# Top-k attention and an ELU feed-forward block on one core: the first two weight pieces on GpSimd's queue, half decoded in the prologue

## The chip, the core and the metric

The kernel runs on one core of a Trainium2 chip. A core has five engines with their own instruction streams: TensorE (PE; its weight loads are shown as PEld), VectorE (DVE), ScalarE (ACT), GpSimd (POOL) and SyncE (SP, which here only issues DMAs). They meet through semaphores. Sixteen DMA engines move data between HBM and the on-chip memory. The metric is the time of one execution on the device, in microseconds; lower is better.

## The reference

```python
# q, k, v: (8, 8, 576, 64)
scores = scale * np.matmul(q, k.transpose(0, 1, 3, 2))
kth = np.partition(scores, -32, axis=-1)[..., -32:-31]
scores = np.where(scores >= kth, scores, -1e9)
attn = softmax(scores)
x = (attn @ v) laid out as (4608, 512)
h = x @ w_in                      # w_in (512, 2048)
g = np.where(h > 0, h, np.exp(np.minimum(h, 0)) - 1)
out = g @ w_out                   # w_out (2048, 512)
```

All arrays but the two weights arrive as 32-bit floats. `w_in` and `w_out` arrive as 64-bit floats, and the kernel turns them into 32-bit floats itself, which is the decoding that this case is about.

## The kernel before

**Attention.** A step of the kernel is one tile of 128 queries (or the 64 left over, for two pairs of heads) of one batch, with one pair of heads. `load_qk` and `load_v` issue the DMAs of a head pair; `transpose_qk` turns q and k on PE and copies them back on ACT (L264, L277); `scores` multiplies them on PE (L301) and copies the result to a tile `sc` on ACT (L309). `select_row` and, later, `select` find the 32 largest of each row on DVE: four times the top eight (MAX8 on L320/L330 or L343/L355) with three replacements between them (L324 or L348). `mask` turns the row into exponentials: two small operations on POOL (L368, L370) and two on ACT (L371, L372). `normalise` works out the reciprocal of the sum on POOL and scales there (L382 to L389). `turn` transposes the result on PE (L408) and copies it on ACT (L409), and `attend` multiplies with v (L434) and puts the result into `xT` (L461).

**Feed-forward.** When a block of tokens has its `xT`, `ffn_pieces` queues its pieces: `hidden` (PE L502, ACT L510 to L513) and `project` (PE L523), with the gate finished on DVE (L478). `feed` takes pieces from this queue four times a step, when the planner's credit allows and when enough weight pieces are decoded (`decoded[0]`).

**Weights.** There are 32 pieces of 128 x 512 numbers, 16 of `w_in` and 16 of `w_out`. `load_weight(i)` fetches the 512 KB of 64-bit words into one of five buffers `raw`, on SP's queue. `convert_first(i)` is the first half of the decoding: three operations on ACT (L170 to L172) and one on POOL (L173). `convert_last(i)` is the second half: two on DVE (L180, L183) and an addition on POOL (L187) that writes `w_in` or `w_out`. `decode_piece(i)` loads piece i + 2, does the first half of piece i and the second half of piece i - 2. Such calls wait in the list `decode`, 34 of them, and `hook` runs one of them at each point in the selection where it is called: twice a step in the first four steps, six times a step in the next four, and three times a step from step 8. When the list is empty, the buffers `raw` are given up for those of the later feed-forward blocks.

**Order.** The first eight steps (`tight = 2 * NHP`) are left to a scheduler of the framework, which may move an instruction of an engine ahead of others when its inputs allow it. Inside `manual_schedule` (a stretch of the prologue that holds the transposes and scores of the first two steps, and everything from step 8 on) the instructions keep the order in which they are written, but those from outside can still be put between them. Each engine then runs its instructions strictly in the order that results, so that one which waits holds up all behind it.

**The prologue.** L628 loads q and k of head pair 0 (k on SP's queue, q on ACT's), L629 weight piece 0, L630 q and k of head pair 1, L631 weight piece 1 and L632 v of head pair 0. L633 to L637 hold the transposes and scores of the first two steps. Then the other q, k and v of batch 0 follow, and L642 fills the list `decode`.

Of the kernel before, what the change touches and what calls it, by code (L numbers as in the profile page):

```python
# [80 lines left out]
def kernel(  # L81
# [9 lines left out]
    nc = tc.nc  # L91
# [9 lines left out]
    NF = dff // P  # L101
# [36 lines left out]
    WN = 512  # L138
    raw = {}

    def weight(i):
        per = dff // WN
        if i < NC * per:
            f, c = divmod(i, NC)
            src = moe_w_in[c * P : (c + 1) * P, 2 * f * WN : 2 * (f + 1) * WN]
            return src, w_in[:, c, f * WN : (f + 1) * WN]
        f = i - NC * per
        return moe_w_out[f * P : (f + 1) * P, :], w_out[:, f, :]

    def load_weight(i):  # L150
        t = rawpool.tile([P, 3 * WN], U32, tag="raw", name="raw")
        nc.sync.dma_start(t[:, 0 : 2 * WN], weight(i)[0])
        raw[i] = t

    def parts(t):
# [3 lines left out]
    def convert_first(i):  # L159

        lo, hi, e = parts(raw[i])
        ef, mf = e.bitcast(FP32), lo.bitcast(FP32)
        nc.scalar.activation(ef, hi.bitcast(FP32), AF.Abs, scale=2.0**-48)  # L170
        nc.scalar.activation(mf, lo, AF.Copy, scale=2.0**-29, bias=2.0**23)
        nc.scalar.activation(lo.bitcast(I32), mf, AF.Copy, bias=-(2.0**23))  # L172
        nc.gpsimd.tensor_scalar(  # L173
            ef, ef, (2.0 - 2.0**-3 - 2.0**-23) * 2.0**-32, 2.0**-63, ALU.min, ALU.max
        )

    def convert_last(i):
        t, dst = raw.pop(i), weight(i)[1]
        lo, hi, e = parts(t)
        nc.vector.tensor_scalar(  # L180
            e, e, 0x0FFFFFFF, 3, ALU.bitwise_and, ALU.logical_shift_left
        )
        nc.vector.scalar_tensor_tensor(  # L183
            out=e, in0=hi, scalar=0x80000000, in1=e,
            op0=ALU.bitwise_and, op1=ALU.bitwise_or,
        )
        nc.gpsimd.tensor_tensor(  # L187
            dst.bitcast(I32), e.bitcast(I32), lo.bitcast(I32), ALU.add
        )

    decode = []
# [13 lines left out]
    def decode_piece(i):  # L205
        if i < 2 * NF:
            if i + 2 < 2 * NF:
                load_weight(i + 2)
            convert_first(i)
        if i > 1:  # L210
            convert_last(i - 2)
            decoded[0] = i - 1
# [3 lines left out]
    def load_qk(b, hp, other=nc.sync):  # L216

        for name, src in (("k", k), ("q", q)):
            n, queue = (J + 1, nc.sync) if name == "k" else (J, other)
            t = ldpool.tile([P, n, 2, D], FP32, tag=name + "in", name=name + "in")  # L220
            if name == "k":
                last = t
            for hh in range(2):
                queue.dma_start(
                    t[:, 0:J, hh, :],
                    src[b, 2 * hp + hh, 0:JP, :].rearrange("(p j) d -> p j d", j=J),
                )
            queue.dma_start(
                last[0:R, J, :, :] if name == "k" else last[R:P, J, :, :],
                src[b, 2 * hp : 2 * hp + 2, JP:S, :].rearrange("h p d -> p h d"),  # L230
            )
            loaded[b, hp, name] = t

    def load_v(b, hp):

        t = kvpool.tile([P, 2 * J + 2, D], FP32, tag="vT", name="vT")
        for hh in range(2):
            h = 2 * hp + hh
            nc.sync.dma_start(
                t[:, hh * J : (hh + 1) * J, :],  # L240
                v[b, h, 0:JP, :].rearrange("(p j) d -> p j d", j=J),
            )
            mine = slice(hh * R, (hh + 1) * R)
            other = slice((1 - hh) * R, (2 - hh) * R)
            nc.gpsimd.memset(t[other, 2 * J + hh, :], 0.0)
            nc.sync.dma_start(t[mine, 2 * J + hh, :], v[b, h, JP:S, :])
        vT[b, hp] = t
# [32 lines left out]
    def start_qk(b, hp):  # L280
        turning.append(transpose_qk(b, hp))

    def turn_qk(whole=False):
        while turning:
            if next(turning[0], turning) is turning:
                turning.pop(0)
            elif not whole:
                return
# [3 lines left out]
    def scores(u):  # L292

        u.sc = scpool.tile([P, 2, S], FP32, tag="sc", name="sc")
        q0 = QUERIES + u.t.qt * P
        for half in range(2):
            for h, i, rows in u.heads:
                kq = kqT[u.t.b, h // 2]
                part = slice(i * D, (i + 1) * D)
                k0 = (KEYS if i == 0 else 0) + half * HS  # L300
                nc.tensor.matmul(  # L301
                    wide[i][rows, half, 0:HS],
                    kq[part, q0 : q0 + u.t.ql],
                    kq[part, k0 : k0 + HS],
                    start=True,
                    stop=True,
                )
        for i in range(2):
            nc.scalar.activation(  # L309
                u.sc[:, i, :].rearrange("p (a s) -> p a s", a=2),  # L310
                wide[i][:, :, 0:HS], AF.Copy, scale=scale,
            )
# [239 lines left out]
    for b in range(B):  # L552
# [12 lines left out]
        for qt in range(J + 1):  # L565
# [8 lines left out]
            t = Tile(b, qt, rows, blk, slice(c0, c0 + n))  # L574
# [21 lines left out]
    def at(step, fn, *args):  # L596
        todo.setdefault(step, []).append((fn, args))
# [28 lines left out]
    E = mybir.EngineType  # L626
    engines = {E.PE, E.Activation, E.DVE, E.Pool}
    load_qk(0, 0, nc.scalar)  # L628
    load_weight(0)  # L629
    load_qk(0, 1)  # L630
    load_weight(1)  # L631
    load_v(0, 0)  # L632
    with tc.manual_schedule(engines=engines):  # L633
        for hp in range(2):
            start_qk(0, hp)
            turn_qk(True)
            scores(steps[hp])  # L637
    load_qk(0, 2)
    load_qk(0, 3)
    for hp in range(1, NHP):  # L640
        load_v(0, hp)
    decode += [lambda i=i: decode_piece(i) for i in range(2 * NF + 2)]  # L642
    at(0, start_qk, 0, 2)
    at(1, start_qk, 0, 3)

# [92 lines left out]
```

## Time and profile before

| | us |
|---|---|
| median of 3 runs (lowest, highest) | 1682.49 (1682.45, 1682.61) |
| the profiled execution | 1682.55 |
| its span, first to last instruction | 1680.8 |
| busy in the span: PE, DVE, ACT, POOL | 1604.5, 1534.4, 1167.5, 638.8 |
| first 15 us, busy: PE, DVE, ACT, POOL | 4.77, 1.54, 6.25, 3.81 |
| 15 to 60 us, busy: PE, DVE, ACT, POOL | 39.41, 44.97, 34.53, 23.16 |
| last 81 us, busy: PE, DVE | 76.73, 5.54 |
| start of step 4's selection on DVE | 58.05 |
| start of step 8's selection on DVE | 146.48 |
| start of step 9's selection on DVE | 158.59 |
| weight loads, issue to landing, lowest, median, highest | 3.1, 3.9, 8.0 |

The busy times are sums of the instructions' durations on each engine, so an engine whose sum is near the length of a stretch has no room in it. A start in the lower rows is the start of the first MAX8 of that step on DVE. A line of a timeline gives start, duration, engine, source line, operation, output and input, a count, and in brackets how long the engine had been idle before it and what ended that.

### The profile page before, as it was taken

The numbers are of one execution on the slowest core, as the hardware profiler recorded it, in microseconds if no ns is written. First come the engines' busy times: TensorE is split into PE (matmuls) and PEld (weight loads), VectorE is DVE, ScalarE is ACT, GpSimd is POOL, SyncE is SP. The second block draws the span as 40 slices with busy tenths as digits, with TensorE's granted clock in tenths as the row PEclk, the third lists the DMA queues.
The fourth block names the chain that finished last, engine by engine and source line by source line (L and its number), as shares of the span: only waits on it lengthen the run. The fifth ranks groups of instructions, "written<-read, shape, count | busy, mean of one in ns | idle before, by whom it ended". The sixth has DMA issues, their size and how long they took to land.

```text
span 1680.8 us, 26396 instructions
## 1 busy us (share of the span) xinstructions
PE 1604.5 (95%) x8560; PEld 1041.7 (62%) x8560; DVE 1534.4 (91%) x3096; ACT 1167.5 (69%) x2661; POOL 638.8 (38%) x1719
## 2 busy tenths in 40 slices
PE   6767999999999999999999999999999999999999
PEld 4554776667575666656557575756558575755565
DVE  6999999999999999999999999999998999998600
ACT  6776786778776776767768685857758586857531
POOL 3776333433333334434334333333333333332200
PEclk8567999999999999999999999999999999999999
DMA  7441021001200111001200111001100000000000
GB/s 192 134 156 39 16 56 36 7 1 47 52 7 7 29 35 42 1 21 36 49 14 1 36 35 42 1 13 43 43 13 8 21 21 29 7 7 7 7 13 13
DMA packets 101129, 56.22 MB, mean 33 GB/s; under 512 B 84097, under 2 KB 92289, under 8 KB 100993
## 3 DMA queue, kind: packets, MB, share of 16 engines
q1 hardware_dynamic: 99792, 54.26, 11.6%
q8 instruction: 68, 1.11, 0.3%
q14 instruction: 69, 0.56, 0.1%
q10 hardware_dynamic: 1200, 0.30, 0.1%
HBM read 45.09 MB, written 9.44 MB: 32 GB/s over the span
## 4 chain that ended last, share of the span: by engine, by line
PE 59%; DVE 26%; ACT 5%; issue 1%; POOL 1%; ACTq 0%; DVEq 0%; POOLq 0%
PE ops L523 22%; PE hps L502 19%; DVE wk L348 11%; DVE m L355 9%; PE avps L434 7%; PE scps L301 6%; PE eps L408 4%; DVE m L343 3%; DVE gT L478 2%; ACT sc L372 1%; ACT sc L371 1%; PE qkps L271 1%; ACT et L409 1%; PE scps L408 1%; ACT n L510 0%
## 5 line engine op out<-in xcount | busy, mean ns | idle before, releaser
L502 PE MATMUL hps<-xT,w_in 128*128 128x256 f32 (+2 forms) x2432 | 557.4, 378 | 25.9 <-ACT gT L511 23.6
L355 DVE MAX8 m<-wk 128x8 f32<-128x576 f32 x816 | 574.5, 744 | 0.0
L523 PE MATMUL ops<-w_out,gT 128*128 128x512 f32 x1152 | 523.8, 599 | 0.0
L502 PEld LDWEIGHTS hps<-xT,w_in 128*128 128x128 f32 x2432 | 411.5, 195 | 127.4 <-ACT gT L511 34.4
L348 DVE MATCH_REPLACE8 wk<-m,wk 128x576 f32<-128x576 f32 x544 | 399.2, 740 | 0.0
L523 PEld LDWEIGHTS ops<-w_out,gT 128*128 128x128 f32 x1152 | 209.0, 190 | 233.6 <-issue 218.7
L382 POOL TENSOR_SCALAR dene<-den 128x2 f32<-128x2 f32 x144 | 34.8, 242 | 832.9 <-ACT sc L372 832.7
L371 ACT ACTIVATE sc<-sc,neg 128x576 f32<-128x576 f32 x288 | 226.4, 786 | 63.2 <-POOL neg L368 63.0
L372 ACT ACTIVATE sc<-sc,gap 128x576 f32<-128x576 f32 x288 | 223.2, 775 | 25.2
L309 ACT ACTIVATE sc<-scps 128x576 f32<-128x576 f32 x288 | 173.6, 662 | 76.6 <-PE scps L301 76.6
L389 POOL TENSOR_SCALAR sc<-sc,rec 128x576 f32<-128x576 f32 x288 | 219.5, 773 | 15.2 <-POOL rec L387 0.6
L409 ACT COPY et<-eps 128x512 f32<-128x512 f32 x288 | 167.5, 582 | 68.4 <-PE eps L408 68.2
L301 PE MATMUL scps<-kqT 64*128 64x288 f32 (+1 forms) x1280 | 200.5, 439 | 15.1 <-ACT kqT L277 8.3
L348 DVE MATCH_REPLACE8 wk<-m,sc 128x576 f32<-128x576 f32 x272 | 199.6, 740 | 0.0
L408 PEld LDWEIGHTS eps<-ident,sc 128*128 128x128 f32 x1152 | 145.1, 145 | 82.9 <-issue 48.0
L478 DVE SCALAR_TENSOR_TENSOR gT<-n,gT 128x512 f32<-128x512 f32 (+2 forms) x152 | 106.5, 701 | 97.7 <-ACT n L513 97.6
L434 PE MATMUL avps<-et,vT 128*64 128x256 f32 (+2 forms) x2080 | 190.4, 326 | 2.7 <-ACT et L409 2.3
L343 DVE MAX8 m<-sc 128x8 f32<-128x576 f32 x272 | 191.0, 742 | 0.0
L408 PE MATMUL eps<-ident,sc 128*128 128x128 f32 x1152 | 178.1, 281 | 12.9 <-POOL sc L389 11.9
L510 ACT ACTIVATE n<-hps 128x256 f32<-128x256 f32 (+2 forms) x304 | 112.6, 370 | 85.5 <-PE hps L502 75.0
L434 PEld LDWEIGHTS avps<-et,vT 128*64 128x64 f32 x2080 | 123.5, 141 | 73.1 <-issue 24.2
L301 PEld LDWEIGHTS scps<-kqT 64*128 64x128 f32 (+1 forms) x1280 | 107.7, 181 | 83.6 <-issue 44.8
(47 smaller groups left out, 1226.8 us busy)
## 6 DMA issues: line engine op xcount, KB each, us to landing
kin<-in_k_dram SPq DMA_DIRECT2D x64, 128.0 KB, 2.8
raw<-in_moe_w_in_dram SPq DMA_DIRECT2D x16, 512.0 KB, 4.4
vT<-in_v_dram SPq DMA_DIRECT2D x64, 128.0 KB, 2.3
raw<-in_moe_w_out_dram SPq DMA_DIRECT2D x16, 512.0 KB, 3.2
out_dram<-osb SPq DMA_DIRECT2D x32, 256.0 KB, 2.3
qin<-in_q_dram SPq DMA_DIRECT2D x62, 128.0 KB, 2.8
kin<-in_k_dram SPq DMA_DIRECT2D x32, 32.0 KB, 2.5
vT<-in_v_dram SPq DMA_DIRECT2D x64, 16.0 KB, 2.2
```

Source lines behind the costliest of these rows:

```text
L301: nc.tensor.matmul(wide[i][rows, half, 0:HS], kq[part, q0 : q0 + u.t.ql], kq[part, k0 : k0 + HS], start=True, stop=True,)
L343: nc.vector.max(found[i], cur[i])
L348: nc.vector.match_replace(wk[i], found[i], cur[i], TAKEN)
L355: nc.vector.max(found[i], cur[i])
L371: nc.scalar.activation(sc, sc, AF.Prelu, bias=neg[:], alpha=STEEP)
L372: nc.scalar.activation(sc, sc, AF.Exp, bias=gap[:], accum_out=u.den[:, i : i + 1])
L389: nc.gpsimd.tensor_scalar(u.sc[:, i, :], u.sc[:, i, :], rec[:, i : i + 1], 1.0, ALU.mult, ALU.mult)
L408: nc.tensor.transpose(ps[:, c * P : (c + 1) * P], sc[:, c0 : c0 + P], ident[:])
L409: nc.scalar.copy(g.et[:, chunks, u.at, :], ps[:, 0 : n * P].rearrange("p (c q) -> p c q", c=n),)
L434: nc.tensor.matmul(ps[i * D : (i + 1) * D, cols], vt[:, 2 * J + i if c == J else i * J + c, :], w, start=(c == 0), stop=(c == J),)
L502: nc.tensor.matmul(ps[:, 0:n_tok], w_in[:, i, f * P : (f + 1) * P], blk.xT[:, i, 0:n_tok], start=(i == 0), stop=(i == NC - 1),)
L523: nc.tensor.matmul(blk.o[:], blk.gT[f // NG][:, f % NG, s * P : (s + 1) * P], w_out[:, f, :], start=(f == 0), stop=(f == NF - 1),)
```

## The change

The loads of weight pieces 0 and 1 are issued on GpSimd's queue, both of them between the loads of q and k of head pair 0 and those of head pair 1. The calls `decode_piece(0)` and `decode_piece(1)` are made in the prologue, after the scores of step 0 and of step 1; as before, such a call loads piece i + 2 on SP's queue and does the first half of piece i. The list `decode` begins with call 2 and has 32 entries instead of 34.

```diff
-    def load_weight(i):
+    def load_weight(i, queue=nc.sync):
         t = rawpool.tile([P, 3 * WN], U32, tag="raw", name="raw")
-        nc.sync.dma_start(t[:, 0 : 2 * WN], weight(i)[0])
+        queue.dma_start(t[:, 0 : 2 * WN], weight(i)[0])
         raw[i] = t
...
     load_qk(0, 0, nc.scalar)
-    load_weight(0)
+    for i in range(2):
+        load_weight(i, nc.gpsimd)
     load_qk(0, 1)
-    load_weight(1)
     load_v(0, 0)
     with tc.manual_schedule(engines=engines):
         for hp in range(2):
             start_qk(0, hp)
             turn_qk(True)
             scores(steps[hp])
+            decode_piece(hp)
     load_qk(0, 2)
     load_qk(0, 3)
     for hp in range(1, NHP):
         load_v(0, hp)
-    decode += [lambda i=i: decode_piece(i) for i in range(2 * NF + 2)]
+    decode += [lambda i=i: decode_piece(i) for i in range(2, 2 * NF + 2)]
```

## The prediction
> **What bounds the kernel now.** I read the slices of the page first, then the busy time by stage, then the two ends of the stretch that the change touches: the timelines of ACT and DVE at the start, and the chain that ended last around 155 us.
>
> ```profile
> 60.00:165.00 105.00, 72.03 (x332) 51.38 (x332) 99.21 (x173) 78.00 (x178) 74.59 (x107) 0.70 0.34 111
> 165.00:400.00 235.00, 219.46 (x1605) 158.07 (x1604) 233.57 (x494) 174.06 (x460) 88.83 (x261) 1.00 0.10 26
> 400.00:1000.00 600.00, 594.09 (x3140) 385.26 (x3139) 593.75 (x1209) 441.60 (x986) 229.91 (x658) 1.00 0.10 27
> 1000.00:1600.00 600.00, 597.96 (x3056) 371.37 (x3053) 555.78 (x1123) 413.69 (x911) 216.49 (x626) 1.00 0.07 18
> ```
> Columns: stage, its length, then busy us of PE, PEld, DVE, ACT, POOL. DVE idles 1.4 us of 235 up to 400 us; PE is the full engine after that. The chain that ended last is DVE alone from 283 us to past 700 us and PE's from about 717 us. So a shift of DVE's work at the start travels to the end, as long as DVE stays without gaps up to there.
>
> The start, on ACT and then on DVE:
> ```profile
> 8.34 0.66 ACT L170 ACTIVATE raw<-raw 128x512 f32<-128x512 f32 x1 [4.29 <-DMA raw<-in_moe_w_in_dram]
> 10.36 1.08 ACT L277 COPY kqT<-qkps 128x512 f32<-128x512 f32 x2
> 13.09 0.66 ACT L170 ACTIVATE raw<-raw 128x512 f32<-128x512 f32 x1 [1.66 <-DMA raw<-in_moe_w_in_dram]
> 14.21 1.17 ACT L309 ACTIVATE sc<-scps 128x576 f32<-128x576 f32 x2
> ...
> 14.57 0.43 DVE L180 TENSOR_SCALAR raw<-raw 128x512 uint32<-128x512 uint32 x1 [3.67 <-POOL raw L173]
> 15.64 1.42 DVE L320 MAX8 m<-sc 128x8 f32<-128x576 f32 x2
> 109.88 1.51 DVE L180 TENSOR_SCALAR raw<-raw 128x512 uint32<-128x512 uint32 x1 [3.46 <-POOL raw L173]
> ```
> ACT stands at piece 0's decode until its load lands (8.34), with q and k already turned on PE; their copies and the first scores come after it, and selection begins at 15.64. The last line is a later wait of DVE for POOL.
>
> The chain in step 8 (start, us, what), and where it returns to DVE:
> ```profile
> 153.47 2.54 issue
> 156.02 1.28 POOL w_out L187
> ...
> 157.39 0.24 POOL dene L382
> ...
> 160.16 1.12 PE eps L408 x4
> ```
> ```profile
> 283.10 0.42 DVE L478 SCALAR_TENSOR_TENSOR gT<-n,gT 128x256 f32<-128x256 f32 x1 [1.43 <-ACT n L513]
> ```
> The last w_out piece stands on POOL ahead of step 7's normalisation, PE idles 5.15 us for it, and the chain runs over PE and ACT until DVE waits 1.43 us at 283 us.
>
> Decode on DVE up to step 9's start (158.59), and the DMA engines early on (share and GB/s last):
> ```profile
> L183 DVE SCALAR_TENSOR_TENSOR raw<-raw 128x512 uint32<-128x512 uint32 x32 | 27.3, 854 | 0.1
> L180 DVE TENSOR_SCALAR raw<-raw 128x512 uint32<-128x512 uint32 x32 | 24.1, 754 | 19.1 <-POOL raw L173 19.1
> ```
> ```profile
> 3.00:6.00 3.00, 0.25 (x2) 0.28 (x3) 0.00 (x0) 1.05 (x1) 0.00 (x0) 1.00 1.04 211
> 6.00:9.00 3.00, 2.12 (x10) 1.71 (x9) 0.00 (x0) 0.66 (x2) 0.00 (x0) 1.00 1.00 257
> ```
> Undisturbed, an L180 takes 0.41 and an L183 0.68 us, so 27.3 - 32 x 0.68 = 5.5 us, 24.1 - 32 x 0.41 = 11.0 us and some 2.3 us of L478 are stretch. Waits for L173 after 15.64 are 19.1 - 9.74 - 3.67 = 5.7 us. Together DVE loses 24.5 us to POOL before step 9, nearly all in steps 4 to 7.
>
> **What the Trainium skill says.** "SBUF — State Buffer", section "SBUF: two separate sides": some DVE operations and GpSimd share a port pair as an exclusive lock for a whole instruction. The trace agrees: an L180 at 58.71 took 1.40 us and ended with the L187 that ran on POOL from 58.54 to 59.83. "DMA: Bandwidth & Descriptors", section "Issuing engines are not separate DMA queues": whoever issues, the same 16 engines move the bytes; their share of 1.0 above says they are full from 3 to 9 us, so a second queue adds no bandwidth there. The same page, section "Queues, rings and completion order": an engine takes turns between queues by packet. Here weights have 4 KB rows, q and k 256 B runs, so POOL's loads would take most of the turns; no run shows it yet. Its section "SWDGE vs HWDGE vs iDMA": GpSimd itself writes the descriptors of its DMAs.
>
> **The change part by part.**
> *Two loads leave SP for POOL.* SP is freed of 0.60 + 0.59 us. POOL issues one load ahead of the identity's last step, which ends at 1.68 and is needed at 5.75. No row shows a POOL issue; I take 1 us for each, with 0 and 4 us as bounds, all hidden behind the next point. q and k of head pair 0 land later, by at most the 2.8 us of engine time of two weight pieces; hidden likewise.
>
> *What ACT really gets.* In the built order of the changed kernel, ACT runs L264, L277 twice, and then L170 to L172 of **piece 2**, ahead of the first scores' L309. Piece 2 is loaded by SP, after q and k of both head pairs and six loads of v. Pieces 0 and 1 do follow the scores. So the wait at the head of ACT isn't removed, it passes from piece 0 to piece 2.
> Its landing: from windows, weights move at about 372 GB/s at full share (365 at 0.98 from 30 us), small runs at about 240 (196 at 0.75, 155 at 0.69). Ahead of and with it go two times 0.59 MB of q and k (4.9 us), 0.44 MB of v (1.8 us) and three pieces of 0.52 MB (4.2 us): 10.9 us. The same sum for before, up to piece 1's landing at 13.09, gives 9.0 where the engines were busy 10.2, so times 1.14: 12.5 us from 2.2 us on, 14.7. By issue: SP has 15 issues ahead of it, of 0.5 to 0.8 us by their rows of before, so 10.1 us, or 11.5 when it waits for landings; plus 4 to 4.7 us as for piece 1: 14.1 to 16.2. I take 15.4, bounds 13.6 and 19. From L170's start, before took 1.9 us to L183's end less POOL's delay; here L170 0.66, L173 0.65, L180 0.43, L183 0.69 and hand-overs give 2.5 us. First MAX8 at 17.9: **+2.3 us** (+0.5 to +5.9).
>
> *Decode in the lead-in.* Before, two pieces (2 x 1.1 us of DVE) fit into the time before 15.64; now one. **+1.1 us.** Two later pieces move from step 8 into the early steps; up to step 9 that sums to nothing, and the work to 158.59 is the same. Scores for step 1 are ready some 5 us before DVE wants them, so nothing more is lost there.
>
> *Waits of DVE for POOL.* In before the third decode of step 6 waits 3.46 us (109.88), since its L173 stands behind step 5's normalisation. In the new order it stands ahead of it. Step 7 keeps the old pattern (1.64 + 0.31). **-3.5 us**, bounds -6.6 and +3; the locks, 18.8 us, are taken as unchanged, for 24 pieces still fall into steps 4 to 7.
>
> *Step 8.* No decode is left there, so L382 follows its L372 at once, some 8 us earlier against DVE, and PE's 5.15 us go. DVE is next late: it has no gap before 283, so only that 1.43 us comes back. **-1.4 us** (0 to -2.1, with 0.66 us at 487). From step 8 on PE's order is the old one.
>
> Sum: 2.3 + 1.1 - 3.5 - 1.4 = -1.5 us. The profiled run took 1682.55 us, its span 1680.8 with 1.75 around it; the median of the runs is 1682.49. So 1681.0.
>
> **The rivals.**
> Slower, by POOL: with the pieces shifted against normalisation, DVE meets POOL's locks and late L173s more often in steps 4 to 7, where POOL is busy 71% (74.59 of 105). The loss goes from 24.5 to 27.5 us: 2.3 + 1.1 + 3.0 - 1.4 = +5.0, **1687.5**. It decides (over +3.4) from 25.9 us on. For it: the loss is large and a matter of phase; against it: the reordered third decode.
> Late landing: piece 2 at 19 us because POOL's packets and SP's own lane waits hold the queue: 5.9 + 1.1 - 3.5 - 1.4 = +2.1, **1684.6**; beyond 20.3 it would be slower. Against it: the saturated sum gives 14.7.
> Faster: piece 2 lands at 13.6 and the loss falls to 17.9 us: 0.5 + 1.1 - 6.6 - 1.4 = -6.4, **1676.1**. For it: in before the decodes of the first four steps show no stretch.
> That the change doesn't do what it says is in all four: its decode lies behind the scores, and a third piece's ahead of them.
>
> **How the numbers follow.** Forecast 0.38; late landing 0.12 (0.08 of it within, 0.04 slower); POOL 0.28; faster 0.22. About 0.2% or 3.4 us is what can be told from no change. Faster 0.22, same 0.46, slower 0.32. The range takes in both outer cases, 1676 to 1689; the likeliest one's own is 1678 to 1685.
>
> **What would show it.** ACT's first L170 waiting for its load at about 15 us with L309 behind it; the first MAX8 near 17.9; no 3.46 us wait in step 6; L382 of step 7 soon after its L372; waits and stretch of DVE between 18 and 28 us up to step 9; step 9 at about 158.5; no wait at 283. A first MAX8 before 14 or after 20, or step 9 off by over 5 us, would make it wrong.

## The result and the profile after

| | before | after |
|---|---|---|
| median of 6 runs (lowest, highest), us | 1682.55 (1681.99, 1683.19) | 1693.77 (1692.89, 1696.07) |
| span of the profiled execution, us | 1680.8 | 1691.4 |
| first product of PE (L259), us | 5.75 | 10.42 |
| first selection on DVE, us | 15.64 | 20.33 |
| start of step 8's selection, us | 146.48 | 159.22 |
| start of step 9's selection, us | 158.59 | 169.21 |

The ratio is 1.0069, with an interval of 1.0057 to 1.0081: the change made the kernel 11.2 us slower, 0.7%. The span grew by 10.6 us and so did the start of step 9, so that all of it is lost before 169 us. What comes after is the old kernel, shifted.

The busy time by stage says the same (stage, its length, busy us of PE, PEld, DVE, ACT and POOL, then PE's clock, the DMA share and GB/s):

```profile
3.00:6.00 3.00, 0.00 (x0) 0.00 (x0) 0.00 (x0) 1.06 (x1) 0.87 (x6) 1.00 0.99 237
6.00:9.00 3.00, 0.00 (x0) 0.00 (x0) 0.00 (x0) 0.00 (x0) 0.00 (x0) 1.00 1.15 323
...
60.00:165.00 105.00, 72.25 (x317) 53.64 (x317) 93.55 (x164) 76.93 (x173) 80.13 (x114) 0.62 0.35 111
165.00:400.00 235.00, 218.00 (x1573) 154.33 (x1572) 233.60 (x494) 171.23 (x452) 84.91 (x254) 1.00 0.09 23
```

From 6 to 9 us no engine computes at all, where PE had been busy for 2.12 us. From 60 to 165 us DVE is busy for 93.55 us instead of 99.21. From 165 us on DVE is full again, as it was.

The start, on ACT:

```profile
11.12 0.32 ACT L264 COPY kqT<-scps 128x192 f32<-128x192 f32 x1 [7.06 <-PE scps L259]
...
17.77 0.66 ACT L170 ACTIVATE raw<-raw 128x512 f32<-128x512 f32 x1 [4.36 <-DMA raw<-in_moe_w_in_dram]
...
19.57 1.18 ACT L309 ACTIVATE sc<-scps 128x576 f32<-128x576 f32 x2
```

The L170 at 17.77 is piece 2's, and the copy of the first scores (L309) stands behind it. PE had these scores ready at 15.75 (eight L301 from 13.46, for 2.29 us). ACT's wait for piece 2 is the last one here, not the late q and k.

DVE, from its first instruction to the long waits in step 4:

```profile
19.26 0.43 DVE L180 TENSOR_SCALAR raw<-raw 128x512 uint32<-128x512 uint32 x1 [19.26 <-POOL raw L173]
...
20.33 1.41 DVE L320 MAX8 m<-sc 128x8 f32<-128x576 f32 x2
...
84.30 0.43 DVE L180 TENSOR_SCALAR raw<-raw 128x512 uint32<-128x512 uint32 x1 [5.27 <-POOL raw L173]
...
89.91 1.51 DVE L180 TENSOR_SCALAR raw<-raw 128x512 uint32<-128x512 uint32 x1 [2.09 <-POOL raw L173]
```

These two waits are new. Before, step 4 (58.05 to 78.16 us) had none. The groups of the decoding on DVE (busy, mean ns, idle before):

```profile
L180 DVE TENSOR_SCALAR raw<-raw 128x512 uint32<-128x512 uint32 x32 | 26.2, 818 | 30.7 <-POOL raw L173 30.7
L183 DVE SCALAR_TENSOR_TENSOR raw<-raw 128x512 uint32<-128x512 uint32 x32 | 24.8, 776 | 0.0
```

Of the 30.7 us, 19.26 are the wait at the very start, before the first selection. So 11.45 us lie after it, against 5.71 before. The stretch of L180 is 26.2 - 32 x 0.41 = 13.1 us, that of L183 24.8 - 32 x 0.68 = 3.0 us and that of L478 2.0 us, together about 0.7 us less than before.

The sum up to step 9: later start 4.69, one decode less ahead of the first selection 1.1, waits 11.45 - 5.71 = 5.74, stretch -0.7. That is 10.8 us, where step 9 moved by 10.62.

What stands behind the wait at 84.30 is read from the chain of waits (start, us, what):

```profile
73.25 2.34 PE avps L434 x18
...
75.61 0.02 ACT xT L461
...
75.77 0.87 ACT sc L372 x2
...
77.90 0.67 ACT sc L371
...
79.61 0.24 POOL dene L382
...
83.66 0.61 POOL raw L173
```

Both exponentials of step 3 (L372) stand on ACT behind the copy L461, which waits for the products L434 of an earlier step. POOL's normalisation of step 3 (L382) waits for the last of these exponentials, and the L173 that DVE wants stands on POOL behind it. It is a loop over three engines that work in order: PE waits for a normalisation, ACT for PE, POOL for ACT, and DVE for POOL. Here L382 begins 12.9 us after the start of step 4's selection (66.68). In the kernel before it began 6.6 us after it (58.05), having waited for ACT for only half a microsecond:

```profile
64.69 0.23 POOL L382 TENSOR_SCALAR dene<-den 128x2 f32<-128x2 f32 x1 [0.52 <-ACT sc L372]
```

### The profile page after: what moved, and what is told of

The parts are those of the page before. It is cut to its first block, busy times and chain, and to the rows that moved or that the text cites. A ratio compares the mean times of both kernels' runs of the same rounds, so it can differ in the third digit from the quotient of the medians.

```text
span 1691.4 us, 26393 instructions
## 1 busy us (share of the span) xinstructions
PE 1606.7 (95%) x8560; PEld 1043.2 (62%) x8560; DVE 1533.5 (91%) x3096; ACT 1168.2 (69%) x2661; POOL 638.7 (38%) x1721
## 3 DMA queue, kind: packets, MB, share of 16 engines
q1 hardware_dynamic: 99504, 53.21, 11.5%
## 4 chain that ended last, share of the span: by engine, by line
PE 65%; DVE 21%; ACT 8%; POOL 2%; issue 2%; DMA 1%; SPq 0%; ACTq 0%; POOLq 0%; DVEq 0%
PE ops L523 24%; PE hps L502 19%; DVE wk L348 9%; PE avps L434 8%; DVE m L355 7%; PE scps L301 7%; PE eps L408 5%; DVE m L343 3%; ACT sc L372 2%; ACT sc L371 1%; DVE gT L478 1%; PE qkps L271 1%; ACT et L409 1%; ACT n L510 1%; PE scps L408 1%
## 5 line engine op out<-in xcount | busy, mean ns | idle before, releaser
L502 PE MATMUL hps<-xT,w_in 128*128 128x256 f32 (+2 forms) x2432 | 559.2, 379 | 28.9 <-ACT gT L511 24.8
L523 PE MATMUL ops<-w_out,gT 128*128 128x512 f32 x1152 | 523.0, 598 | 0.0
L382 POOL TENSOR_SCALAR dene<-den 128x2 f32<-128x2 f32 x144 | 35.0, 243 | 842.9 <-ACT sc L372 842.8
L523 PEld LDWEIGHTS ops<-w_out,gT 128*128 128x128 f32 x1152 | 208.6, 190 | 233.2 <-issue 218.5
L372 ACT ACTIVATE sc<-sc,gap 128x576 f32<-128x576 f32 x288 | 223.4, 776 | 25.3
L309 ACT ACTIVATE sc<-scps 128x576 f32<-128x576 f32 x288 | 173.9, 661 | 82.1 <-PE scps L301 82.1
L301 PE MATMUL scps<-kqT 64*128 64x288 f32 (+1 forms) x1280 | 201.2, 442 | 8.9 <-ACT kqT L277 3.7
L478 DVE SCALAR_TENSOR_TENSOR gT<-n,gT 128x512 f32<-128x512 f32 (+2 forms) x152 | 106.4, 700 | 97.5 <-ACT n L513 97.5
L434 PE MATMUL avps<-et,vT 128*64 128x256 f32 (+2 forms) x2080 | 191.2, 327 | 2.7 <-ACT et L409 2.4
L434 PEld LDWEIGHTS avps<-et,vT 128*64 128x64 f32 x2080 | 123.6, 142 | 73.4 <-issue 26.1
L301 PEld LDWEIGHTS scps<-kqT 64*128 64x128 f32 (+1 forms) x1280 | 108.0, 182 | 77.7 <-issue 46.3
```

The costliest lines, as they stand in the source:

```text
L301: nc.tensor.matmul(wide[i][rows, half, 0:HS], kq[part, q0 : q0 + u.t.ql], kq[part, k0 : k0 + HS], start=True, stop=True,)
L372: nc.scalar.activation(sc, sc, AF.Exp, bias=gap[:], accum_out=u.den[:, i : i + 1])
L434: nc.tensor.matmul(ps[i * D : (i + 1) * D, cols], vt[:, 2 * J + i if c == J else i * J + c, :], w, start=(c == 0), stop=(c == J),)
L502: nc.tensor.matmul(ps[:, 0:n_tok], w_in[:, i, f * P : (f + 1) * P], blk.xT[:, i, 0:n_tok], start=(i == 0), stop=(i == NC - 1),)
L523: nc.tensor.matmul(blk.o[:], blk.gT[f // NG][:, f % NG, s * P : (s + 1) * P], w_out[:, f, :], start=(f == 0), stop=(f == NF - 1),)
```

## The experiments

Three theories were tested. START: q and k land later, or ACT waits longer for a weight piece, and the selections begin later by that much. QUEUE: loads on GpSimd's queue in themselves make later work late, in POOL or in the transfers. ORDER: with the loads elsewhere the scheduler puts the early steps into another order, and the waits come from that order. In the expectations of the first four runs ORDER is narrower: it means only the order of the decode pieces in steps 4 to 7. It was widened to the order on all engines after these runs. Fifteen kernels ran on the chip. In all, as in the two kernels of the case, the span is the start of step 9 on DVE plus 1522.0 to 1522.9 us. A kernel is therefore judged by that start. Times and ratios are medians of several executions; starts and waits are those of the one profiled execution.

The first four take the change apart. **q_only** is the queue alone (`load_weight` takes the queue as in the change):

```diff
--- the kernel before
-    load_weight(0)
-    load_qk(0, 1)
-    load_weight(1)
+    for i in range(2):
+        load_weight(i, nc.gpsimd)
+    load_qk(0, 1)
```

> Only the queue of the loads of pieces 0 and 1 is changed (GpSimd's); the decoding stays in the hooks. Theory START (the end moves by as much as the start of step 9 on DVE, and the start of the first MAX8 is set by loads): q and k of head pair 0 land late again, first transpose near 10.4 us, first MAX8 at 16.5 to 17.5 instead of 15.64, time 1683.5 to 1686. Rival QUEUE (the software queue is the whole loss): 1691 or more. Rival ORDER (the loss is the new order of decode pieces in steps 4 to 7): 1681 to 1685, with DVE's waits for L173 after the first MAX8 near 6 us.

Measured: 1692.27 us, ratio 1.006 (1.0045 to 1.0075), almost all of the loss. First product at 10.85 us; first selection at 16.89, 1.25 us later than before, since before ACT stood at piece 1's load until 13.09 anyway; step 9 at 168.03, 9.4 us later. Some 8 us are lost after the start. 6.89 of them are one wait in step 4, on DVE and then on POOL:

```profile
79.11 1.51 DVE L180 TENSOR_SCALAR raw<-raw 128x512 uint32<-128x512 uint32 x1 [6.89 <-POOL raw L173]
```
```profile
73.67 0.23 POOL L382 TENSOR_SCALAR dene<-den 128x2 f32<-128x2 f32 x1 [4.89 <-ACT sc L372]
```

It has the form of the wait in the changed kernel: the normalisation of step 3 is late on POOL because ACT's exponentials are. Of the expected times only QUEUE's, 1691 us or more, came.

The traces show that the order did change. Up to step 9 q_only runs the same instructions as the kernel before, but for the two issues on POOL. DVE has its 253 in the same order; PE, ACT and POOL have theirs in another one. On ACT, around the exponentials of step 2, before and then in q_only:

```profile
46.32 0.78 ACT L372 ACTIVATE sc<-sc,gap 128x576 f32<-128x576 f32 x1
...
49.91 0.76 ACT L372 ACTIVATE sc<-sc,gap 128x576 f32<-128x576 f32 x1
...
51.78 0.27 ACT L461 COPY xT<-avps 128x128 f32<-128x128 f32 x1
```
```profile
54.89 0.27 ACT L461 COPY xT<-avps 128x128 f32<-128x128 f32 x1 [1.05 <-PE avps L434]
55.05 0.78 ACT L372 ACTIVATE sc<-sc,gap 128x576 f32<-128x576 f32 x1
...
58.16 0.77 ACT L372 ACTIVATE sc<-sc,gap 128x576 f32<-128x576 f32 x1
```

Before, the copy L461 stood behind both exponentials; in q_only they stand behind it, and it waits for PE.

**p_only** is the prologue's decoding alone:

```diff
--- the changed kernel
-    for i in range(2):
-        load_weight(i, nc.gpsimd)
-    load_qk(0, 1)
+    load_weight(0)
+    load_qk(0, 1)
+    load_weight(1)
```

> Only the decoding is moved into the prologue; pieces 0 and 1 are loaded on SP's queue where they were. START: first transpose near 5.8 us, first scores copied before any decoding, first MAX8 at 10.5 to 12.5; 4 us earlier less 2.2 us for two decodes that no longer lie ahead of it; time 1679 to 1682 if DVE's waits stay near 6 us. QUEUE: as fast as before or faster, 1679 to 1683. ORDER: waits of DVE for L173 near 11 us, time 1684 to 1688 in spite of the early start.

Measured: 1684.58 us, ratio 1.0014 (1.0008 to 1.0021). The first selection is at 12.02 us, with no decode ahead of it. Two decodes take 2 x 1.1 us, so 15.64 - 12.02 - 2.2 = 1.4 us are gained. Waits for L173 take 10.82 us instead of 5.71, stretch is 1.7 us less, and step 9 is 1.8 us later than before. This is what ORDER expected. The calls do what they are meant to do when piece 2 doesn't stand ahead of L309, and their gain is lost in waits.

**late23** takes the loads of pieces 2 and 3 out of the prologue and puts them behind all q, k and v:

```diff
--- the changed kernel
-            decode_piece(hp)
+            convert_first(hp)
...
+    load_weight(2)
+    load_weight(3)
     decode += [lambda i=i: decode_piece(i) for i in range(2, 2 * NF + 2)]
```

> The changed kernel with the loads of pieces 2 and 3 moved behind the loads of q, k and v of batch 0, so that piece 2 can't stand on ACT ahead of the first scores; pieces 0 and 1 stay on GpSimd's queue. START: first transpose still near 10.4, first MAX8 near 16.4 instead of 20.3, 3.9 us less, one decode more behind it (1.1 us): 1690 to 1692 if nothing else moves. QUEUE: 1692 to 1695. ORDER: depends on the new waits alone, time after minus the fall of the waits from 11.4 us.

Measured: 1695.82 us, ratio 1.008 (1.0065 to 1.0095). With piece 2 no longer ahead of L309 the first selection is at 16.92 us instead of 20.33. What is left of the delay against p_only, 4.9 us, is that of q and k (first product at 10.87 against 5.97). The earlier start isn't kept: there is a wait of 7.75 us in step 4, and step 9 is at 173.11. START's 1690 to 1692 us and QUEUE's 1692 to 1695 were both passed.

**empty2** gives the changed kernel the old cadence of the list, so that hook n does again what it does in the kernel before:

```diff
--- the changed kernel
+    decode += [lambda: None] * 2
     decode += [lambda i=i: decode_piece(i) for i in range(2, 2 * NF + 2)]
```

> The changed kernel with two empty entries at the head of the list, so that every later decode comes in the hook in which it came before. START: first MAX8 at 20.3, waits much as in the changed kernel, 1691 to 1695. ORDER: the same start, waits for L173 fall from 11.4 to about 6 us, 1687 to 1690. QUEUE: 1692 to 1695.

Measured: 1699.22 us, ratio 1.0109 (1.0091 to 1.0127); waits of 5.23 and 3.84 us in step 4, step 9 at 172.79. All three expectations were lower. The old cadence doesn't bring the old time back, so the new cadence alone isn't the cause.

After these four a large wait in step 4 and GpSimd's queue went together in every run. Two readings were left, the queue or the order. The next four keep the order of the first eight steps as it is written, by moving one line, and combine it with the two parts of the change:

```diff
--- in m_before, m_q, m_p and m_after alike
+    ctx.enter_context(tc.manual_schedule(engines=engines))
     for n in range(NS + 3):
...
-        if n == tight:
-            ctx.enter_context(tc.manual_schedule(engines=engines))
```

> The kernel before with the order of its first eight steps also kept as it is written, instead of left to the framework's scheduler. It is the base for the next run: only the difference between the two is to be read. Against the kernel before, no theory has a number: START says that the end is the start of step 9 on DVE plus 1522 to 1523 us here too, whatever step 9's start is; first product of PE at 5.8 us as before.

> The same fixed order, with the loads of pieces 0 and 1 on GpSimd's queue ahead of q and k of head pair 1. The instructions of PE, DVE and ACT stand in the same order as in the run before. ORDER (most of the 10 us of the queue-only run come from the order that the scheduler makes when the loads are on GpSimd's queue): only the later start is left, first product of PE at 10.4 to 10.9 us, first selection later by 1 to 5 us, no new wait in step 4, and 1 to 5 us slower than the fixed order with SP's loads. QUEUE (the loads on GpSimd's queue themselves make POOL or the transfers late): the 5 to 8 us wait of DVE for POOL's L173 around step 4 is there as well, and the run is some 10 us slower than the fixed order with SP's loads.

> The same fixed order, with the first two calls of decode_piece in the prologue behind the scores and all loads on SP's queue. START: first selection near 12 us as in the run with the prologue's decoding alone, and one decode fewer ahead of it, so about 1 to 2 us faster than the fixed order of before if the waits stay as they are. ORDER: the gain is kept here, since no scheduler can place the decoding differently; rival (the cadence of the list, two hooks earlier, is what costs): waits of DVE for L173 rise by 3 to 6 us as in the scheduled run with the prologue's decoding alone, and it is 1 to 4 us slower than the fixed order of before.

> The whole change in the fixed order. ORDER: against the fixed order with the prologue's decoding on SP's queue, only the later start is left: first product at 10.4 us, first selection later by 3 to 6 us, time longer by the same 3 to 6 us. QUEUE: longer by 8 to 12 us, with a wait of over 4 us in step 4.

| | time, us | first product | first selection | waits in step 4 | step 9 |
|---|---|---|---|---|---|
| m_before | 1724.13 | 6.10 | 12.14 | 5.20 + 1.96 | 199.93 |
| m_q (queue) | 1729.17 | 10.39 | 16.43 | 5.20 + 1.96 | 205.00 |
| m_p (decoding) | 1726.52 | 6.14 | 12.19 | 1.16 + 5.20 + 1.96 | 202.25 |
| m_after (both) | 1730.22 | 11.04 | 17.09 | 0.77 + 5.20 + 1.96 | 207.03 |

All four are 2.5% to 2.9% slower than the kernel before (ratios 1.0251 to 1.0286), so the scheduler's order is worth some 42 us. What counts here are the differences. In m_before and m_q the instructions of PE, DVE and ACT stand in the same order. On DVE, first m_before, then m_q:

```profile
75.71 1.51 DVE L180 TENSOR_SCALAR raw<-raw 128x512 uint32<-128x512 uint32 x1 [5.20 <-POOL raw L173]
81.43 1.50 DVE L180 TENSOR_SCALAR raw<-raw 128x512 uint32<-128x512 uint32 x1 [1.96 <-POOL raw L173]
```
```profile
79.99 1.52 DVE L180 TENSOR_SCALAR raw<-raw 128x512 uint32<-128x512 uint32 x1 [5.20 <-POOL raw L173]
85.73 1.50 DVE L180 TENSOR_SCALAR raw<-raw 128x512 uint32<-128x512 uint32 x1 [1.96 <-POOL raw L173]
```

The waits are the same to a hundredth, and 4.3 us later, by as much as the first selection is. With the order fixed the queue costs 5.04 us: 4.29 at the start and 0.8 later: in step 8 a wait for the gate's exponential (L513) grows from 5.86 to 6.93 us, and one in step 6 shrinks by 0.29. QUEUE had expected 10, ORDER 1 to 5. A wait of 5.20 us in step 4 comes here without any load on GpSimd's queue. The decoding costs 2.4 us in the fixed order, where START and ORDER expected a gain: in m_before no decode stands ahead of the first selection (12.14) to begin with. The rival of two earlier hooks had this time (1 to 4 us), but not its waits: those for L173 after the first selection grew by 0.7 us, not by 3 to 6. What makes up the rest of the 2.4 us stays open. m_after took 3.7 us more than m_p, within ORDER's 3 to 6, and 6.1 us more than m_before.

One limit: m_before has long waits of its own. The four show that the queue adds none to them in this order. GpSimd's queue in the very order of the kernel before was not run.

The next three look for the wait in scheduled kernels on SP's queue, and one halves the dose.

```diff
--- wlate, against the kernel before
-    load_weight(0)
     load_qk(0, 1)
-    load_weight(1)
     load_v(0, 0)
...
+    load_weight(0)
+    load_weight(1)
     decode += [lambda i=i: decode_piece(i) for i in range(2 * NF + 2)]
--- late23_sp, against late23
-    for i in range(2):
-        load_weight(i, nc.gpsimd)
     load_qk(0, 1)
+    for i in range(2):
+        load_weight(i)
--- p_empty2, against p_only
+    decode += [lambda: None] * 2
     decode += [lambda i=i: decode_piece(i) for i in range(2, 2 * NF + 2)]
--- q_one, against q_only
-    for i in range(2):
-        load_weight(i, nc.gpsimd)
+    load_weight(0, nc.gpsimd)
     load_qk(0, 1)
+    load_weight(1)
```

> The kernel before, with pieces 0 and 1 still on SP's queue but loaded behind all q, k and v of batch 0; the decoding as before. GpSimd issues no load. The built order of POOL has, as in the queue-only run, no L173 between step 3's last mask and its normalisation (L382). ORDER: DVE waits 5 to 8 us for POOL's L173 in step 4 all the same; first product at 5.8 us, first selection near 12 us without a decode ahead of it, step 9 at about 165 us, time about 1687 to 1690 us. QUEUE: without GpSimd's queue no wait over 2 us in step 4, and 1680 to 1684 us.

> The run that loads pieces 2 and 3 late, with pieces 0 and 1 on SP's queue behind q and k of head pair 1 instead of on GpSimd's ahead of them. Here an L173 does stand between step 3's last mask and its L382. ORDER: no wait over 2 us in step 4 (the same source with GpSimd's queue had 7.75), tail waits of 1 to 2 us as in the run with the prologue's decoding alone; first selection near 12 us, step 9 at about 160 us, time 1682 to 1685 us. QUEUE gives the same here; a wait over 4 us in step 4 would go against ORDER.

> The prologue's decoding alone, on SP's queue, with two empty entries at the head of the list, so that the hooks from the third on do what they do in the kernel before. POOL's built order has no L173 between step 3's last mask and its L382. ORDER: a wait of 5 to 8 us in step 4 without GpSimd's queue; first selection near 12 us, step 9 at 162 to 165 us, time 1685 to 1688 us. QUEUE (and the rival that two earlier hooks are what costs in the run without GpSimd): no wait over 2 us in step 4, the start's gain is kept, 1679 to 1682 us.

> The queue-only run with piece 0 alone on GpSimd's queue and piece 1 on SP's behind q and k of head pair 1. START, if q and k wait for the bytes of the loads on GpSimd's queue: one load instead of two gives about half of the delay, first product of PE at 7.5 to 9 us (5.75 with none, 10.85 with two). If the delay is that of a second queue at all, not of its bytes: 10 us or later. ORDER: the same order of DVE as in the queue-only run and the same wait of 5 to 8 us in step 4; first selection at 15.5 to 17 us, time 1688 to 1692 us. QUEUE: half of the loss, about 1687 us.

p_empty2 shows that the long wait doesn't need that queue: no load on GpSimd's queue, first product at 6.00 us, first selection at 12.04, and the longest wait of all in step 4, on DVE and POOL:

```profile
80.34 1.51 DVE L180 TENSOR_SCALAR raw<-raw 128x512 uint32<-128x512 uint32 x1 [8.11 <-POOL raw L173]
```
```profile
74.92 0.23 POOL L382 TENSOR_SCALAR dene<-den 128x2 f32<-128x2 f32 x1 [4.47 <-ACT sc L372]
```

It took 1693.31 us, ratio 1.0069 (1.0054 to 1.0084), as long as the change, from nearly the earliest start of all. ORDER had expected the wait, but only 1685 to 1688 us. From p_only it differs by the two empty entries alone, and they cost 8.7 us. late23_sp took 1684.9 us (1.0017, 1.0009 to 1.0024), without a wait in step 4, as ORDER expected. wlate missed what ORDER expected: 1686.62 us (1.0027, 1.0016 to 1.0038) and only 2.25 us of wait; it missed QUEUE's 1680 to 1684 us as well. The sign used to foretell it, an L173 between step 3's last mask and its L382, isn't enough. q_one, 1694.24 us (1.0073, 1.0058 to 1.0088), had its first product at 9.30 us, a little past START's 7.5 to 9; one trace doesn't settle whether the delay goes with the bytes. Its time is above all that was expected. Its first selection was at 20.29, because ACT stood at piece 1's load until 14.30 with the copies of q and k behind it.

wlate put another sign in place of that one: how late POOL begins the normalisation of step 2, counted from the start of step 3's selection. The last three kernels test it, with two more orders that have a second queue. hook2_q is hook2 with the loads of q_only; q_scalar is the changed kernel with ACT's queue.

```diff
--- hook2, against the kernel before
-    decode += [lambda i=i: decode_piece(i) for i in range(2 * NF + 2)]
+    for i in range(2):
+        decode_piece(i)
+    decode += [lambda i=i: decode_piece(i) for i in range(2, 2 * NF + 2)]
--- q_scalar, against the changed kernel
-        load_weight(i, nc.gpsimd)
+        load_weight(i, nc.scalar)
```

> The kernel before with the first two calls of decode_piece made ahead of the list, but not inside the prologue's hand-ordered part, and all loads on SP's queue: the two earlier hooks alone. START: the first selection stays near 15.6 us with two decodes ahead of it, since ACT's decoding stays where it was. ORDER: the normalisation of step 2 begins less than 6 us after the start of step 3's selection, as in all runs so far without a long wait in step 4, and then no wait over 3 us in step 4; step 9 at 156 to 160 us, time 1680 to 1684 us. Rival (two earlier hooks are what costs): waits and stretch of DVE 4 us or more above the kernel before, time 1685 us or more.

> The same with pieces 0 and 1 on GpSimd's queue ahead of q and k of head pair 1; another scheduled order with that queue. All five scheduled kernels with that queue so far had a wait of 5 to 8 us in step 4. ORDER: the wait over 4 us is there only if the normalisation of step 2 begins more than 8 us after the start of step 3's selection; if it begins less than 6 us after it, the wait is under 3 us and the run is 1 to 5 us slower than the one without the queue. QUEUE: the wait is there whatever that lag is, and the run is some 10 us slower than the one without the queue.

> The whole change with the two loads on ACT's queue, where ACT issues them right behind q of head pair 0, instead of on GpSimd's. START, if the start is lost to 1 MB of weights moving beside q and k: first product of PE at 8 to 11 us here too. If it is lost because the two loads go out ahead, at 1.3 us, or by GpSimd's kind of queue: 6 to 7 us here. ORDER: another order; a wait over 4 us in step 4 only if step 2's normalisation begins more than 8 us after the start of step 3's selection. QUEUE (GpSimd's queue itself): no wait over 3 us.

hook2 took 1685.15 us (1.002, 1.0012 to 1.0028): the wait in step 4 is small (1.70), as the sign says, and still step 9 is 2.9 us late, so the time is a little over what ORDER gave and in the range of its rival, two earlier hooks. The rival's waits and stretch were to grow by 4 us or more; they grew by 1.8 and 1.1. hook2_q took 1690.63 us (1.0051, 1.0036 to 1.0066), 5.5 us more than hook2, with 3.44 us of wait in step 4; its lag of 7.1 us falls between the two limits of the expectation. q_scalar took 1695.05 us (1.0077, 1.006 to 1.0094), with first product at 8.16 us and waits of 3.79 and 3.71 us in step 4, without GpSimd's queue. Both START and ORDER allowed for this, QUEUE did not.

All scheduled kernels in order of the lag (us; lag of the normalisation L382 of steps 2 and 3 after the start of the next step's selection; waits of DVE for L173 within step 4, and that step's length; in brackets the decodes ahead of the first selection; the time is the median, all else is from one profiled execution, whose time is up to 2.5 us off the median):

| kernel | extra queue | time | first selection | lag, step 2 | lag, step 3 | waits in step 4 | its length | step 9 |
|---|---|---|---|---|---|---|---|---|
| wlate | none | 1686.62 | 12.09 (0) | 4.1 | 7.7 | 2.25 | 20.5 | 161.60 |
| before | none | 1682.55 | 15.64 (2) | 4.3 | 6.6 | 0 | 20.1 | 158.59 |
| p_only | none | 1684.58 | 12.02 (0) | 4.6 | 9.0 | 1.41 | 20.5 | 160.39 |
| late23_sp | none | 1684.90 | 12.55 (0) | 4.6 | 7.4 | 0 | 19.1 | 160.95 |
| hook2 | none | 1685.15 | 15.88 (2) | 5.5 | 6.4 | 1.70 | 21.7 | 161.49 |
| hook2_q | GpSimd | 1690.63 | 16.59 (2) | 7.1 | 9.8 | 3.44 | 21.8 | 166.86 |
| after | GpSimd | 1693.77 | 20.33 (1) | 8.9 | 12.9 | 7.36 | 26.7 | 169.21 |
| q_scalar | ACT | 1695.05 | 19.75 (1) | 9.0 | 12.6 | 7.50 | 26.1 | 171.11 |
| empty2 | GpSimd | 1699.22 | 20.58 (1) | 10.0 | 13.9 | 9.23 | 30.3 | 172.79 |
| q_one | GpSimd, one | 1694.24 | 20.29 (2) | 10.2 | 11.6 | 5.31 | 23.5 | 168.85 |
| q_only | GpSimd | 1692.27 | 16.89 (2) | 11.7 | 13.2 | 7.10 | 25.8 | 168.03 |
| late23 | GpSimd | 1695.82 | 16.92 (0) | 11.9 | 14.2 | 7.75 | 26.2 | 173.11 |
| p_empty2 | none | 1693.31 | 12.04 (0) | 13.8 | 17.3 | 10.62 | 29.9 | 170.08 |

Where step 2's normalisation comes within 5.5 us, DVE waits at most 2.25 us in step 4; where it comes after 8.9 us or more, it waits 5.3 to 10.6 us; hook2_q lies between. This holds with and without a second queue. The lag shows the mechanism; it isn't known beforehand, since it is the outcome of the built order on PE, ACT and POOL.

Part of it can be read from that order. The second copy L461 on ACT stands behind both exponentials of step 2 in three of these kernels (before, late23_sp, hook2), and they wait 0 to 1.70 us in step 4. It stands ahead of both in five (after, empty2, q_one, q_only, p_empty2), and they wait 5.31 to 10.62 us. In the other five it stands between them, and the waits are 1.41 to 7.75 us. No run changed this place alone, and the four kernels with the fixed order, where it stands behind both, wait 7.2 to 8.3 us, so it isn't the whole rule.

A slower TensorE is an obvious rival, since the clock granted to it was 0.62 in the mean from 60 to 165 us, against 0.70 before. It doesn't explain the lag of step 2: from the start of that step's selection to its L382 the clock was 0.50 before (34.93 to 50.86 us), with a lag of 4.3 us, and 0.69 in the changed kernel (41.99 to 64.07 us), with 8.9. What it adds to the later waits isn't known.

Why the scheduler takes the worse order in six of the seven scheduled kernels with a second queue stays open: no run looked into the scheduler. No kernel tried beats the kernel before.

## Why the prediction was wrong

It said 1681.0 us, no change, with 1676 to 1689 as range. By its own steps:

**The start, +2.3 us: right in its place, too small.** It was seen that ACT would stand at piece 2's load ahead of the first scores. The landing was taken at 15.4 us and came at 17.77, so that the term measured 4.69 us, within its bounds. With 20.33 us the first selection still passed the 20 us that the prediction had named as a sign of being wrong. The missing 2.4 us are SP's. On SP's queue, in the changed kernel (start, us of issuing):

```profile
5.94 3.00 SPq L224 DMA_DIRECT2D qin<-in_q_dram  x2
8.99 0.91 SPq L228 DMA_DIRECT2D kin<-in_q_dram  x1
...
13.41 1.06 SPq L152 DMA_DIRECT2D raw<-in_moe_w_in_dram  x2
```

Two issues of q took 3.00 us, where they took 1.28 us before, and piece 2 went out at 13.41 us. The sum by issues had 10.1 to 11.5 us. The landing, 4.36 us after that, was as taken.

**q and k later by at most 2.8 us, hidden: wrong in size, right in effect.** The first product came 4.67 us later. The bound was the engine time of two pieces at full rate, but small transfers beside large ones lost more than that. From the DMA issues of the changed kernel, and then of the kernel before (KB each, median us from issue to landing):

```profile
raw<-in_moe_w_in_dram POOLq DMA_DIRECT2D x2, 512.0 KB, 6.9
...
qin<-in_q_dram ACTq DMA_DIRECT2D x2, 128.0 KB, 4.9
kin<-in_q_dram ACTq DMA_DIRECT2D x1, 32.0 KB, 6.7
```
```profile
qin<-in_q_dram ACTq DMA_DIRECT2D x2, 128.0 KB, 3.1
kin<-in_q_dram ACTq DMA_DIRECT2D x1, 32.0 KB, 3.3
```

The prediction cited the Trainium skill, "DMA: Bandwidth & Descriptors", section "Queues, rings and completion order": an engine takes one packet from each queue in turn. From this it follows that large packets get most of the bytes, not most of the turns, as the prediction put it. The trace agrees: from 3 to 9 us POOL's queue had 285 of 2885 packets, but 1.04 of 1.68 MB and 57.9% of the engines' time. The prediction also said that a second queue adds no bandwidth while the engines are full: in these 6 us, full in both kernels, they moved 1.68 MB instead of 1.40. In the changed kernel the delay is hidden, since the scores were ready at 15.75 and ACT waited for piece 2 until 17.77. In late23, q_only and m_q it isn't.

**The decode in the lead-in, +1.1 us:** one piece instead of two, as said.

**Waits of DVE for POOL, -3.5 us: this is the step that failed.** They grew by 5.74 us, and with -0.7 us of stretch the loss went from 24.5 to about 29.5 us. The locks, taken as unchanged, were so within this 0.7 us. (The L180 at 58.71 us, which it read as ending with POOL's L187, ended 0.28 us after it, at 60.11.) The prediction looked at one wait, the 3.46 us in step 6, saw from the built order that its L173 now stood ahead of a normalisation, and counted that as a gain. That wait did go; in step 6 there are only 0.60 us now. But the order of POOL alone doesn't say when an L382 can run: it waits for ACT's exponentials, and these for PE. The loop over PE, ACT and POOL that delays step 3's normalisation to 79.61 us was in the built order as well and was not followed. The rival "slower, by POOL" had the place and the sign, with 27.5 us of loss and 1687.5 us; it was given 0.28. It was too small in the waits by 2 us and took the start from the forecast.

How much of the 11.2 us is the order's can be estimated from the fixed order, where the queue alone costs 5.04 us, the whole change 6.1 us, and the waits in step 4 grow by 0.8 us at most. That leaves 5 to 6 us for the order, the size of the new waits. It is worked out across kernels, not measured in the changed kernel itself.

**Step 8, -1.4 us: the first half came, the gain didn't.** No decode was left in step 8, and POOL began step 7's normalisation (L382) at 161.22 us, less than a microsecond after its L372; PE's wait of 5.15 us is gone. But DVE's wait of some 1.4 us came back at the same distance from step 9. On DVE, after:

```profile
293.82 0.43 DVE L478 SCALAR_TENSOR_TENSOR gT<-n,gT 128x256 f32<-128x256 f32 x1 [1.40 <-ACT n L513]
```

293.82 - 169.21 = 124.6 us, and before 283.10 - 158.59 = 124.5; in wlate, 286.24 - 161.60 = 124.6. The wait belongs to the pattern of work behind step 9, and PE's idle time in step 8 wasn't what fed it. With 169.21 us step 9 missed the expected 158.5 by more than the 5 us that the prediction allowed itself. In the changed kernel PE spent that time on 16 products L523 that took 7.57 us at 158.87.

## What to carry to other kernels

That the consumer of a bulk load can wait doesn't make the load free on a second queue: first find which small transfers move in the same microseconds and who starts from them. Where a scheduler orders the code, moving a load is also a change of order; follow each late normalisation or decode through all engines that stand ahead of it in the built order, not along one engine. To tell the load from the order, compare two builds whose order is kept by hand, look only at their difference, and ask whether that order already has the wait that you look for.

## What was not expected of the hardware

- Two loads of 512 KB on GpSimd's queue (issued at 1.3 and 2.4 us in the changed kernel) held the first product of PE to between 10.4 and 11.0 us in all seven kernels that had both, whatever else changed. One load held it to 9.30, and two on ACT's queue, issued at 2.78 us behind q, to 8.16 us; of these two there is one trace each.
- Without a second queue the first product came at 5.75 to 6.5 us, but at 7.47 us in hook2, whose issues on SP up to 6.9 us are those of the kernel before, within 0.01 us. So a difference of one or two microseconds in a single early landing proves nothing, and the 8.16 and 9.30 above lie within that of hook2's 7.47.
- In one fixed order the first five waits of DVE for L173, in steps 4 and 5, repeated from m_before to m_q within 0.02 us while everything had shifted by 4.3 us. The later ones differ: in step 6 one went from 5.62 to 5.33 us.
